# Leftover transposes of an attention pair: two parts in two successive slots of the pipeline

## The chip, the cores and the metric

One program runs on one core of a Trainium2 chip. The metric is the time of one execution on the device in microseconds (us), the median of the runs. The core has a matrix engine (PE, with its weight loads listed apart as PEld), a vector engine (DVE), a scalar engine (ACT), POOL, and SP, which here issues transfers. Each engine works through its own instructions in order, and they wait for each other by semaphores.

## What is computed

An attention with a cut at a threshold, for 8 batches of 8 heads, 576 positions and 64 columns, and then eight experts to which 4608 rows are given out greedily by their logits.

```python
scores = scale * np.matmul(q, k.transpose(0, 1, 3, 2))
thresh = np.max(scores, axis=-1, keepdims=True) - tau
scores = np.where(scores >= thresh, scores, -1000000000.0)
scores = scores - np.max(scores, axis=-1, keepdims=True)
attn = np.exp(scores)
attn = attn / (np.sum(attn, axis=-1, keepdims=True) + 1e-09)
return np.matmul(attn, v).astype(np.float32)
...
h = np.maximum(x[mask] @ w1[e], 0.0)
out[mask] = h @ w2[e]
```

## The kernel before, in words

The attention comes first and is all that the change touches; the routing and the experts follow, and start from what the last attention tiles give.

**Tiles and pairs.** Two heads make a pair `p`; there are 32 pairs, four to a batch. A pair has nine tiles of 128 query rows by 576 keys: tiles 0 to 7 are four for each head, tile 8 holds the last 64 rows of both. So there are 288 tiles, numbered through: `p,i=divmod(t,9)`.

**One tile's way.** `score` (line 69, PE) writes the scores of the tile into a score tile `sc`, `[128,2,512]` in PSUM, two banks, of which columns 0 to 287 of each bank are used. `mx` (line 74, DVE) scales it into `z` and takes the row's extreme; line 75 (POOL) adds `tau` to it. `ex` (line 86, ACT) takes the exponent into `pp` (`pm` for tile 8), and `stt` (line 90, DVE) sets to zero what lies under the threshold and sums. `tr` (line 98, PE, by the helper `turn`) transposes keys 0 to 511 of the tile into the bank tile `tb`; `trev` (lines 113 and 115, ACT) copies that into `pt`. `pv_unit` (line 144, PE) multiplies by the values into `xo`.

**The leftover.** Keys 512 to 575 are transposed apart, for the whole pair at once: `left` (by `turn`, so line 98 again, but out to `sc`) writes ten transposes into the columns from 288 on of score tiles that hold scores at the time. Its first part (n=0) is six transposes, of tiles 0 to 5; its second part (n=1) is four, two of tiles 6 and 7 and two of tile 8 (`pm`). `leftev` (ACT) copies them into `pl`: line 123 the first part (128x384), line 126 (128x128) and twice line 127 (64x64) the second. `pl_unit` (line 152, PE) multiplies `pl` by its values and closes the sum in `xo`; line 153 (ACT) copies `xo` to `xt` at the start of the next slot.

**Slots.** The loop over `s_` does two tiles of each stage in a slot: scores of tiles 2s+4 and 2s+5, `stt` of 2s+2 and 2s+3, `tr` of 2s and 2s+1, `trev` of 2s-2 and 2s-1. The order in which a slot's calls are written is the order on every engine: on PE the two scores, then units of the queue (`columns`, `whole`: `pv_unit`, `pl_unit`, units for the logits and for rows), then `tr`; on ACT first what `flush` has kept from the slot before (among it line 153), then two `trev`, then two `ex`; on DVE two `mx`, two `stt`, then copies of units. There are two score tiles (`ps_s`, bufs=2), so a slot's first score waits until the first score tile of the slot before has been read, and its second score until the second has; and one `tb` (`ps_t`, bufs=1) for both tiles of a slot, so a slot's `tr` waits for both `trev` of that slot.

**Where the leftover stands.** A pair's tile 8 is transposed by `tr` in one slot, called A here, and copied by `trev` in the next, called B. Before, both parts of `left` stand in slot B: the first behind the first score, in that score's tile; the second behind the second score, in its tile. All four copies of `leftev` stand in slot B too, ahead of both exponents. Nine slots hold two pairs. For an even `p` tile 8 is the first of its slot's two tiles, for an odd `p` the second.

Of the kernel before, what the change touches and what calls it, by code (L numbers as in the profile page):

```python
# [13 lines left out]
AF = mybir.ActivationFunctionType  # L14
# [8 lines left out]
def attention(ctx, tc, qk, vl, tau, wgd, xrows, xts, Lg, nb_batches, ident, swap, R, after_first):  # L23
# [14 lines left out]
    def load(p):  # L38
        b,j=divmod(p,4)
        x=ld.tile([128,QK],F32,name="qk"); v=ld.tile([128,2,S],F32,name="vt",bufs=VTB)  # L40
        if p==0:

            a=HS+128; h=HS+S
            for q,c,e in ((nc.sync,0,a),(nc.scalar,h,h+a),(nc.sync,a,h),(nc.scalar,h+a,QK)):
                q.dma_start(x[:,c:e], qk[b,j,:,c:e])
                if c==0: nc.sync.dma_start(taub, bass.AP(tensor=tau.tensor,offset=tau.offset,ap=[[0,128],[1,1]]))
        else: nc.sync.dma_start(x, qk[b,j])
        nc.sync.dma_start(v, vl[b,j])
        t={"v":v}; c=0
        for n,w in ((("k",0),HS),(("q",0),S),(("k",1),HS),(("q",1),S)):  # L50
            t[n]=x[:,c:c+w]; c+=w
        LD[p]=t
# [7 lines left out]
    def score(t):  # L60

        p,i=divmod(t,9); kd=LD[p]
        sc=ps_s.tile([128,2,512],F32,name="sc"); SC[t]=sc
        if i<8: todo=((i%2,slice(0,128),slice(i//2*128,i//2*128+128)),)
        else: todo=((0,slice(0,64),slice(512,576)),(1,slice(64,128),slice(512,576)))
        for h,o,c in todo:
            for f in range(2):
                r=slice(64*f,64*f+64)
                T.matmul(sc[o,f,:HS], kd["q",h][r,c], kd["k",h][r,:],start=True,stop=True)  # L69
    ZB={}  # L70
    def mx(t):
        nb=wk.tile([128,2],F32,name="nb",bufs=6); NBI[t]=nb
        z=wk.tile([128,2,HS],F32,name="z",bufs=5); ZB[t]=z
        V.tensor_scalar(z,SC.pop(t)[:,:,:HS],-0.125,None,op0=ALU.mult,op1=ALU.min,accum_out=nb[:,0:1])  # L74
        G.tensor_scalar(nb[:,1:2],nb[:,0:1],taub[:,0:1],None,op0=ALU.add)  # L75
# [3 lines left out]
    def pview(t):  # L79
        p,i=divmod(t,9)  # L80
        if i==8: return PM[p%2][:,D:D+S]
        k=(p,i//2)
        if k not in PB: PB[k]=wk.tile([128,2,S],F32,name="pp",bufs=PPB)
        return PB[k][:,place(i)]
    def ex(t):
        A.activation(pview(t),ZB[t].rearrange("p a b -> p (a b)"),AF.Exp,bias=NBI[t][:,0:1],scale=-1.0)  # L86
    def stt(t):
        p,i=divmod(t,9)
        pv=pview(t)
        V.scalar_tensor_tensor(pv,ZB.pop(t).rearrange("p a b -> p (a b)"),NBI[t][:,1:2],pv,op0=ALU.is_le,op1=ALU.mult,accum_out=den_of(p)[:,p%4,i:i+1])  # L90
# [5 lines left out]
    def turn(o,*x):  # L96
        for r in range(2):
            g=slice(64*r,64*r+64); T.transpose(o[:,r],x[r%len(x)][g],ident[g,g])  # L98
# [4 lines left out]
    def tr(t,first):  # L103
        p,i=divmod(t,9)
        tb=bank(t,first)
        pv=pview(t)
        o=(64,0) if i==8 else (64*place(i),)*2
        for kb in range(4): turn(tb[:,:,kb],*(pv[:,c+kb*128:c+(kb+1)*128] for c in o))
    def trev(t):
        p,i=divmod(t,9); tb=TB.pop(t)  # L110
        if i==0: PT[p]=wk.tile([128,2,4,S],F32,name="pt"); PL[p]=wk.tile([128,S],F32,name="pl")
        if i<8:
            A.activation(PT[p][:,i%2,:,(i//2)*128:(i//2+1)*128].rearrange("p k (r q) -> p r k q",r=2),tb,AF.Copy)  # L113
        else:
            A.activation(PT[p][:,:,:,512:576],tb,AF.Copy)
    LB={}
    def left(p,n,t):
        sc=SC[t] if t is not None else ps_s.tile([128,2,512],F32,name="sc")
        LB[p,n]=sc
        for g in ((0,1,2),(3,))[n]: turn(sc[:,:,HS+64*(g%3):HS+64*(g%3)+64],PB[p,g].rearrange("p a b -> p (a b)")[:,512:640])  # L120
        if n: turn(sc[:,:,HS+64:HS+128],PM[p%2][:,0:128],PM[p%2][:,S:S+128])
    def leftev(p,n):
        if n==0: a=LB.pop((p,0)); A.activation(PL[p][:,0:384].rearrange("p (g r q) -> p r g q",g=3,r=2),a[:,:,HS:HS+192].rearrange("p r (g q) -> p r g q",g=3),AF.Copy)  # L123
        if n==0: return
        b=LB.pop((p,1))
        A.activation(PL[p][:,384:512].rearrange("p (r q) -> p r q",r=2),b[:,:,HS:HS+64],AF.Copy)
        for r in range(2): A.activation(PL[p][64-64*r:128-64*r,512:576],b[64-64*r:128-64*r,r,HS+64:HS+128],AF.Copy)  # L127


    have={}  # L130
# [93 lines left out]
    def push_pair(p):  # L224
        b,j=divmod(p,4)
        def when(n): return lambda: have.get((p,n),1<<30)+HOLD<=st["slot"]
        if p==NP-1:


            def left(f):  # L230
                for k,g in pl_unit(p,(f,)): g(); k[0]=True
            for f in range(2):
                for u in range(4): queue.append(("c",when("t3" if f==0 else "t8"),u==0,lambda f=f,u=u: pv_unit(p,f,u),p))
                if f==0: queue.append(("n",when("t8"),False,lambda: rd_calc(b),p))
            for g in (lambda: left(0),lambda: left(1),lambda: lg_unit(b,0)(),lambda: lg_unit(b,1)(),lambda: lgt_unit(b)(),lambda: lgm_unit(b)()):
                queue.append(("n",when("pl"),False,g,p))
            queue.append(("n",lambda: not later,False,lambda: late.extend([lambda c=c: xt_unit(b,c) for c in range(5)]),p))
            return
        for f in range(2):
            for u in range(4): queue.append(("c",when("t3" if f==0 else "t8"),u==0,lambda f=f,u=u: pv_unit(p,f,u),p))  # L240
            if (f,j)==(0,3): queue.append(("n",when("t8"),False,lambda: rd_calc(b),p))
        queue.append(("c",when("pl"),False,lambda: pl_unit(p),p))
        if (b,j)==(0,0): queue.append(("n",lambda: True,False,R.consts,p))
        if (b,j)==(nb_batches-1,2): queue.append(("n",lambda: not aux,False,lambda: (R.prep(0,28),R.compare(R.k("E1"),J,0,28)),p))
        if j==3: queue.append(("n",lambda: not later,False,lambda: finish(b),p))
# [7 lines left out]
    def flush():  # L253
        for k,g in later: g(); k[0]=True
        later.clear()
    def last_slot(p): return 9*(p//2)+(12 if p%2 else 8)
    def columns(all=False):
        c=[x[4] for x in queue if x[0]=="c"]
        if not c: n=9
        else: n=9 if all else max(1,c.count(c[0])//max(1,last_slot(c[0])-st["slot"]+1))  # L260
        while queue and queue[0][1]():
            k,_,first,g,p=queue[0]
            if k=="c":
                if n==0: return
                if first and (not free_v() or (not all and not XO and len(aux)>(3 if p%2 else 0) and st["held"]!=p)): return
                n-=1
            queue.pop(0); r=g()
            if k=="c" and r:
                later.extend(r)
                return  # L270
    def whole():
        n=0
        while n<2 and aux and not XO and free_v() and st["slot"]>=st["last"]+aux[0][0]:
            r=aux.pop(0)[1](); n+=1; st["last"]=st["slot"]
            if queue: st["held"]=queue[0][4]
            later.append((banks[-1],r))
# [10 lines left out]
    for s_ in range(-2,NT//2+2):  # L287
        st["slot"]=s_
        sc_=[t for t in (2*s_+4,2*s_+5) if 0<=t<NT]; tr_=[t for t in (2*s_,2*s_+1) if 0<=t<NT]
        ev_=[t for t in (2*s_-2,2*s_-1) if 0<=t<NT]; tt_=[t for t in (2*s_+2,2*s_+3) if 0<=t<NT]  # L290
        p8=[t//9 for t in ev_ if t%9==8]
        for n in range(2):
            if n<len(sc_): score(sc_[n])
            for p in p8: left(p,n,sc_[n] if n<len(sc_) else None)

        flush()
        for t in ev_:
            p,i=divmod(t,9)
            while i==0 and p>1 and (p-2,"pv") not in have: columns(True); flush()
            trev(t); have[p,f"t{i}"]=s_  # L300
        if ev_ and ev_[-1]==NT-1: columns(True)
        for t in ev_:
            p,i=divmod(t,9)
            if i==3: push_pair(p)
            if i==8: have[p,"pl"]=s_
        for t in sc_: mx(t)
        for n in range(2):
            for p in p8: leftev(p,n)
        for t in sc_: ex(t)
        for t in tt_: stt(t)  # L310
        for t in sc_:
            p,i=divmod(t,9)
            if i==8 and p+2<NP: load(p+2)
        columns(); whole()
        for t in tr_: tr(t,t==tr_[0])
# [4 lines left out]
    for k in range(0,NBO,2):  # L320
        bk=wk.tile([128,2,4,S],F32,name="pt")
        for i in range(min(2,NBO-k)):
            b=nb_batches-NDEF-NBO+k+i; XT[b]=bk[:,i]; nc.sync.dma_start(XT[b],xts[b])
# [633 lines left out]
```

## Time and profile before

| | us |
|---|---|
| median of 3 runs | 1012.78 |
| lowest, highest of the runs | 1012.51, 1014.81 |
| the profiled execution: its own time | 1014.5 |
| its span, first to last instruction | 1012.7 |
| PE busy | 960.3 |
| PEld busy | 704.5 |
| DVE busy | 784.7 |
| ACT busy | 639.1 |
| POOL busy | 258.7 |

The trace counts from the first instruction, so the profiled execution has 1.8 us outside its span. The attention fills the span up to about 480 us: the last `tr` starts at 475.1 us, the last line 152 at 480.1 us. The rest is the routing, the first expert's start and the experts. The granted TensorE clock is 0.99 over the span.

### The profile page before, as it was taken

The numbers are of one execution on the slowest core, as the hardware profiler recorded it, in microseconds if no ns is written. First come the engines' busy times: TensorE is split into PE (matmuls) and PEld (weight loads), VectorE is DVE, ScalarE is ACT, GpSimd is POOL, SyncE is SP. The second block draws the span as 40 slices with busy tenths as digits, with TensorE's granted clock in tenths as the row PEclk, the third lists the DMA queues.
The fourth block names the chain that finished last, engine by engine and source line by source line (L and its number), as shares of the span: only waits on it lengthen the run. The fifth ranks groups of instructions, "written<-read, shape, count | busy, mean of one in ns | idle before, by whom it ended". The sixth has DMA issues, their size and how long they took to land.

```text
span 1012.7 us, 24106 instructions
## 1 busy us (share of the span) xinstructions
PE 960.3 (95%) x9141; PEld 704.5 (70%) x9141; DVE 784.7 (77%) x2158; ACT 639.1 (63%) x1257; POOL 258.7 (26%) x411
## 2 busy tenths in 40 slices
PE   7999999999999999999879999999999899999996
PEld 4555555555555555555669789797887879899895
DVE  7999999999999899997578788788687687525220
ACT  6898889788988889897745344254352444535340
POOL 2333433333333333232020222221221203220202
PEclk9999999999999999999979999999999999999999
DMA  6332424233432323202770523434343415351101
GB/s 247 98 116 83 140 81 157 99 135 124 169 115 95 102 101 118 95 26 88 245 250 13 170 97 121 136 114 128 124 138 115 143 50 177 93 174 53 42 11 41
DMA packets 35859, 116.99 MB, mean 116 GB/s; under 512 B 4384, under 2 KB 5024, under 8 KB 35232
## 3 DMA queue, kind: packets, MB, share of 16 engines
q1 hardware_dynamic: 28352, 92.85, 26.8%
q0 software_dynamic: 5888, 19.03, 6.0%
q10 hardware_dynamic: 1504, 3.59, 1.2%
q8 instruction: 72, 1.18, 0.5%
q14 instruction: 43, 0.35, 0.1%
HBM read 93.01 MB, written 21.38 MB: 113 GB/s over the span
## 4 chain that ended last, share of the span: by engine, by line
PE 69%; DVE 12%; ACT 10%; issue 6%; DMA 2%; another core or an unknown queue 0%; DVEq 0%; POOLq 0%; SPq 0%; ACTq 0%
PE pf L787 21%; PE pf L819 19%; PE xo L144 8%; PE sc L69 8%; PE tb L98 6%; DVE z L74 4%; ACT pp L86 4%; DVE pp L90 3%; ACT pt L113 3%; PE xo L152 2%; PE pt L732 2%; ACT pl L127 1%; PE rps L440 1%; PE xo L205 1%; DMA out_dram<-y,idx 1%
## 5 line engine op out<-in xcount | busy, mean ns | idle before, releaser
L75 POOL TENSOR_SCALAR nb<-nb,taub 128x1 f32<-128x1 f32 x288 | 149.4, 519 | 308.3 <-DVE z L74 257.6
L74 DVE TENSOR_SCALAR_CACHE_REDUCE z<-sc 128x576 f32<-128x576 f32 x288 | 205.9, 752 | 26.8 <-PE sc L69 14.1
L86 ACT ACTIVATE pp<-z,nb 128x576 f32<-128x576 f32 x256 | 186.4, 771 | 23.6 <-DVE z L74 23.6
L90 DVE SCALAR_TENSOR_TENSOR pp<-z,nb,pp 128x576 f32<-128x576 f32 x256 | 199.9, 813 | 0.3
L819 PE MATMUL pf<-w2h,H 128*128 128x512 f32 x576 | 195.3, 402 | 0.7 <-DVE H L372 0.7
L69 PE MATMUL sc<-qk 64*128 64x288 f32 (+1 forms) x1280 | 186.4, 427 | 7.2 <-ACT pl L123 2.7
L144 PE MATMUL xo<-pt,vt 128*64 128x320 f32 (+1 forms) x1024 | 151.1, 418 | 3.4 <-PE sc L69 1.2
L113 ACT ACTIVATE pt<-tb 128x512 f32<-128x512 f32 x256 | 139.0, 588 | 5.2 <-PE tb L98 2.2
L819 PE MATMUL pf<-w2l,H 128*128 128x512 f32 x320 | 128.3, 401 | 0.0
L826 POOL DMA_INDIRECT out_dram<-y,idx x40 | 44.6, 1115 | 314.6 <-ACT y L822 238.6
L98 PEld LDWEIGHTS tb<-ident,pp 64*128 64x128 f32 x2048 | 75.0, 139 | 69.6 <-ACT pt L113 28.0
L819 PEld LDWEIGHTS pf<-w2h,H 128*128 128x128 f32 x576 | 106.5, 189 | 20.2 <-DVE H L372 1.6
L69 PEld LDWEIGHTS sc<-qk 64*128 64x128 f32 (+1 forms) x1280 | 91.1, 178 | 34.3 <-ACT pl L127 9.0
L787 PE MATMUL pf<-xh,w1h 128*128 128x288 f32 (+2 forms) x512 | 110.7, 303 | 0.7 <-ACT xh L733 0.7
L144 PEld LDWEIGHTS xo<-pt,vt 128*64 128x64 f32 x1024 | 63.4, 136 | 68.4 <-issue 34.7
L787 PE MATMUL pf<-xh,w1l 128*128 128x288 f32 (+2 forms) x512 | 110.7, 302 | 0.0
L787 PE MATMUL pf<-xl,w1h 128*128 128x288 f32 (+2 forms) x512 | 110.6, 302 | 0.0
L98 PE MATMUL tb<-ident,pp 64*128 64x64 f32 x2048 | 93.9, 229 | 12.3 <-ACT pt L113 12.0
L822 ACT ACTIVATE y<-pf 128x512 f32<-128x512 f32 x40 | 23.9, 598 | 129.3 <-PE pf L819 121.1
L799 ACT ACTIVATE hf<-pf 128x576 f32<-128x576 f32 x56 | 36.5, 652 | 93.2 <-PE pf L787 80.3
L787 PEld LDWEIGHTS pf<-xh,w1h 128*128 128x128 f32 x512 | 82.6, 191 | 1.5 <-ACT xh L733 1.1
L787 PEld LDWEIGHTS pf<-xh,w1l 128*128 128x128 f32 x512 | 82.6, 191 | 0.2
(199 smaller groups left out, 1311.4 us busy)
## 6 DMA issues: line engine op xcount, KB each, us to landing
qk<-qk_dram SPq DMA_DIRECT2D x31, 864.0 KB, 4.9
vt<-vl_dram SPq DMA_DIRECT2D x32, 576.0 KB, 3.8
w2s<-w_dram SPq DMA_DIRECT2D x32, 512.0 KB, 5.3
w1s<-w_dram SPq DMA_DIRECT2D x28, 512.0 KB, 4.3
xrows<-pp SPq DMA_DIRECT2D x24, 260.0 KB, 2.3
xts<-xt SPq DMA_DIRECT2D x2, 1152.0 KB
pt<-xts SPq DMA_DIRECT2D x2, 1152.0 KB, 7.9
xrows<-xr SPq DMA_DIRECT2D x8, 260.0 KB, 2.4
```

The source lines that it names most:

```text
L69: T.matmul(sc[o,f,:HS], kd["q",h][r,c], kd["k",h][r,:],start=True,stop=True)
L74: V.tensor_scalar(z,SC.pop(t)[:,:,:HS],-0.125,None,op0=ALU.mult,op1=ALU.min,accum_out=nb[:,0:1])
L75: G.tensor_scalar(nb[:,1:2],nb[:,0:1],taub[:,0:1],None,op0=ALU.add)
L86: A.activation(pview(t),ZB[t].rearrange("p a b -> p (a b)"),AF.Exp,bias=NBI[t][:,0:1],scale=-1.0)
L90: V.scalar_tensor_tensor(pv,ZB.pop(t).rearrange("p a b -> p (a b)"),NBI[t][:,1:2],pv,op0=ALU.is_le,op1=ALU.mult,accum_out=den_of(p)[:,p%4, ...
L98: g=slice(64*r,64*r+64); T.transpose(o[:,r],x[r%len(x)][g],ident[g,g])
L113: A.activation(PT[p][:,i%2,:,(i//2)*128:(i//2+1)*128].rearrange("p k (r q) -> p r k q",r=2),tb,AF.Copy)
L144: T.matmul(xo[64*h:64*h+64,:q.stop-q.start],v[:,f,128*u+64*h:128*u+64*h+64],PT[p][:,h,u,q],start=(u==0),stop=False,skip_group_check=True)
L787: T.matmul(ps[:,h,:n],s[w][:,k,f*128:(f+1)*128],s[x][:,k,cols[h]],start=(i==0),stop=(i==11))
L799: A.activation(hf,ps[:,:,:HS],AF.Relu)
L819: T.matmul(ps[:,0,:],H[:,f,c:c+128],s[w][:,f],start=(f==0 and j==0),stop=e)
L826: G.indirect_dma_start(out=out,out_offset=IOA(ap=s["idx"][:n,t:t+1],axis=0),in_=y[:n],in_offset=None)
```

## The change

The first part of `left` moves from slot B to slot A, behind both scores of that slot, and writes into the second score's tile. The second part stays in slot B behind both scores, in the second score's tile as before. `leftev` follows its part: line 123's copy now stands in slot A and lines 126 and 127 in slot B, each between the two exponents of the slot. The work itself, its shapes and its number are the same.

```diff
-        p8=[t//9 for t in ev_ if t%9==8]
-        for n in range(2):
-            if n<len(sc_): score(sc_[n])
-            for p in p8: left(p,n,sc_[n] if n<len(sc_) else None)
+        p8=[(t//9,n) for n,x in enumerate((tr_,ev_)) for t in x if t%9==8]
+        for t in sc_: score(t)
+        for p,n in p8: left(p,n,sc_[-1] if sc_ else None)
...
         for t in sc_: mx(t)
-        for n in range(2):
-            for p in p8: leftev(p,n)
-        for t in sc_: ex(t)
+        for t in sc_[:1]: ex(t)
+        for p,n in p8: leftev(p,n)
+        for t in sc_[1:]: ex(t)
```

`leftev` is written anew with the same four copies; lines from there on shift by two, later by one, so line 123 becomes 125, lines 126 and 127 become 127 and 128, and lines 144 and 152 become 146 and 154.

On PE, this is the start of slot A of an even pair before (the names in brackets are the semaphores waited for):

```order
L69 MATMUL sc<-qk 128x288 [waits DVE_49]
L69 MATMUL sc<-qk 128x288
L69 MATMUL sc<-qk 128x288 [waits DVE_49]
L69 MATMUL sc<-qk 128x288
L144 MATMUL xo<-pt,vt 64x320 x4
```

and now:

```order
L69 MATMUL sc<-qk 128x288 [waits DVE_49]
L69 MATMUL sc<-qk 128x288
L69 MATMUL sc<-qk 128x288 [waits DVE_49]
L69 MATMUL sc<-qk 128x288
L98 MATMUL sc<-ident,pp 128x64 x6
L146 MATMUL xo<-pt,vt 64x320 x4
```

The six transposes of the first part have come in behind the two scores and ahead of the multiplication by the values. The same pair's slot B on PE before (`pm_101` is its tile 8):

```order
L69 MATMUL sc<-qk 128x288 [waits DVE_49]
L69 MATMUL sc<-qk 128x288
L98 MATMUL sc<-ident,pp 128x64 x6
L69 MATMUL sc<-qk 128x288 [waits DVE_49]
L69 MATMUL sc<-qk 128x288
L98 MATMUL sc<-ident,pp 128x64 x2
L98 MATMUL sc<-ident,pm_101 128x64 x2
```

and now:

```order
L69 MATMUL sc<-qk 128x288 [waits DVE_49]
L69 MATMUL sc<-qk 128x288
L69 MATMUL sc<-qk 128x288 [waits Activation_49]
L69 MATMUL sc<-qk 128x288
L98 MATMUL sc<-ident,pp 128x64 x2
L98 MATMUL sc<-ident,pm_101 128x64 x2
```

They have gone from between the two scores of slot B, whose second score now waits for a copy of ACT's: the first part's, in slot A.

On ACT, slot B of an even pair and the first copies of the slot behind it, before:

```order
L115 ACTIVATE pt<-tb 128x8x64 [waits PE_49]
L113 ACTIVATE pt<-tb 128x2x4x64 [waits Activation_49]
L123 ACTIVATE pl<-sc 128x2x3x64 [waits DVE_49]
L126 ACTIVATE pl<-sc 128x128 [waits DVE_49]
L127 ACTIVATE pl<-sc 64x64 x2
L86 ACTIVATE pp<-z,nb 128x576 x2
L113 ACTIVATE pt<-tb 128x2x4x64 [waits PE_49]
L113 ACTIVATE pt<-tb 128x2x4x64
```

and now, from the exponents of slot A on (line 178, 176 before, is a copy for the logits that `flush` has kept):

```order
L86 ACTIVATE pp<-z,nb 128x576 [waits DVE_49]
L125 ACTIVATE pl<-sc 128x2x3x64 [waits DVE_49,Activation_49]
L86 ACTIVATE pp<-z,nb 128x576
L178 ACTIVATE lt<-xo 128x320 [waits PE_49]
L115 ACTIVATE pt<-tb 128x8x64 [waits PE_49]
L113 ACTIVATE pt<-tb 128x2x4x64 [waits Activation_49]
L86 ACTIVATE pp<-z,nb 128x576 [waits DVE_49]
L127 ACTIVATE pl<-sc 128x128 [waits DVE_49]
L128 ACTIVATE pl<-sc 64x64 x2
L86 ACTIVATE pp<-z,nb 128x576
L113 ACTIVATE pt<-tb 128x2x4x64 [waits PE_49]
L113 ACTIVATE pt<-tb 128x2x4x64
```

In slot B one exponent now stands ahead of the copies of the leftover and one behind, and the largest of the copies is gone to slot A, between that slot's exponents. The first score of the slot behind B, which waited for ACT's line 123, now waits for DVE's `mx` alone. The order on DVE is the same in both kernels, and so are the transfers of SP and the work of POOL.

More of the change, by code (lines that the diff above doesn't have):

```diff
@@ L122, in leftev @@
     def leftev(p,n):
[L123 to L127, printed above, removed]
+        sc=LB.pop((p,n))
+        if n==0:
+            A.activation(PL[p][:,0:384].rearrange("p (g r q) -> p r g q",g=3,r=2),sc[:,:,HS:HS+192].rearrange("p r (g q) -> p r g q",g=3),AF.Copy)
+            return
+        A.activation(PL[p][:,384:512].rearrange("p (r q) -> p r q",r=2),sc[:,:,HS:HS+64],AF.Copy)
+        for r in range(2): A.activation(PL[p][64-64*r:128-64*r,512:576],sc[64-64*r:128-64*r,r,HS+64:HS+128],AF.Copy)
     have={}
```

## The prediction

> **What bounds the kernel now.** I read the table by stretches first, then the groups of the page, the list of waits, the chain of waits, and last the timeline of one slot B and the slot behind it. The columns of the stretch: its length, then busy time and count of PE, PEld, DVE, ACT and POOL, the granted clock, the transfers' share and GB/s.
>
> ```profile
> 25.00:475.00 450.00, 431.27 (x5157) 251.15 (x5157) 425.10 (x1211) 392.57 (x750) 150.72 (x294) 1.00 0.31 104
> L74 DVE TENSOR_SCALAR_CACHE_REDUCE z<-sc 128x576 f32<-128x576 f32 x288 | 205.9, 752 | 26.8 <-PE sc L69 14.1
> PE tb L98 <- ACT pt L113: 8.3, 22, 0.6
> PE sc L69 <- ACT pl L123: 2.5, 4, 0.8
> PE sc L69 <- ACT pl L127: 1.3, 8, 0.2
> PE tb L98 <- ACT pt L113: 1.4, 5, 0.5
> ```
>
> In the attention PE is busy 431 of 450 us and DVE 425: two engines near full that take turns in setting the pace. The second row says where DVE loses time: 26.8 us of idle time ahead of line 74, over the whole span, waiting for PE. The last four are PE's waits (total, times, longest); the first three hold for 60 to 470 us, the last for 25 to 60 us. PE idles 8.3 us in 22 waits ahead of the transposes into `tb`, for ACT's copies out of it.
>
> ```profile
> 449.30 0.50 ACT pl L123
> ...
> 451.22 0.76 ACT pp L86
> 451.98 0.97 ACT pt L113 x2
> 452.99 0.71 PE tb L98 x16
> ```
>
> The chain that ended last runs through this place: line 123's copy, the other copies of the leftover, an exponent, two copies of `pt`, then `tb`. So ACT's work in slot B does set the end, though ACT as a whole is the emptiest of the three.
>
> **One slot B and the slot behind it.** Start, length, what; in brackets the idle time ahead and who ended it.
>
> ```profile
> 402.59 0.76 DVE L74 TENSOR_SCALAR_CACHE_REDUCE z<-sc 128x576 f32<-128x576 f32 x1 [0.67 <-PE sc L69]
> 407.16 0.76 DVE L74 TENSOR_SCALAR_CACHE_REDUCE z<-sc 128x576 f32<-128x576 f32 x1
> 407.85 0.08 DVE L74 DVE_READ_ACCUMULATOR z<-sc 128x1 f32 x1
> 407.96 0.49 ACT L123 ACTIVATE pl<-sc 128x384 f32<-128x384 f32 x1 [2.15 <-DVE z L74]
> 408.64 0.28 ACT L126 ACTIVATE pl<-sc 128x128 f32<-128x128 f32 x1 [0.19 <-DVE z L74]
> 408.93 0.45 ACT L127 ACTIVATE pl<-sc 64x64 f32<-64x64 f32 x2
> 409.28 1.43 ACT L86 ACTIVATE pp<-z,nb 128x576 f32<-128x576 f32 x2
> 410.61 1.06 ACT L113 ACTIVATE pt<-tb 128x512 f32<-128x512 f32 x2
> 408.50 0.76 PE L69 MATMUL sc<-qk 64*128 64x288 f32 x4 [0.76 <-ACT pl L123]
> 409.43 0.71 PE L69 MATMUL sc<-qk 64*64 64x288 f32 x8 [0.17 <-ACT pl L127]
> 410.07 1.08 PE L144 MATMUL xo<-pt,vt 128*64 128x256 f32 x8
> 411.72 0.71 PE L98 MATMUL tb<-ident,pp 64*128 64x64 f32 x16 [0.56 <-ACT pt L113]
> 412.27 1.19 PE L69 MATMUL sc<-qk 64*128 64x288 f32 x8
> 413.39 1.30 PE L144 MATMUL xo<-pt,vt 128*64 128x320 f32 x8
> ```
>
> The copies of the leftover hold ACT from 407.96 to 409.38; both exponents follow, from 409.28; only then come the two copies of `pt`, done at 411.67, and `tb` starts at 411.72. PE could have started it at 411.08: its work of line 144 ends at 411.15, and a group starts some 0.07 us before the end of the one ahead (412.27 + 1.19 = 413.46, the next starts at 413.39). This wait so costs 0.56 + 0.07 = 0.63 us.
>
> **The change, part by part.** No work is added or taken away; four things move.
>
> The exponent ahead of the copies. The first exponent needs `z` alone. The first row's accumulator has been read at 407.93, so it starts at 407.96, where line 123 starts now. One exponent takes the queue for 1.43 - 0.76 = 0.67 us, to 408.63: the time at which line 126 starts anyway, once the second `z` is done (408.64). Lines 126 and 127 stay where they are, to 409.38; the second exponent starts at 409.28, where the first does now; the copies of `pt` start 0.67 us earlier, at 409.94, and end at 411.00; ACT would allow `tb` at 411.05, PE at 411.08. The second score keeps its wait for line 127 (409.43). So `tb` starts at 411.08, and the whole wait of 0.63 us is gone; ACT has given 0.67, so no wait of these 22, whose longest is 0.6, is left. **8.3 + 22 x 0.07 = 9.8 us** of PE time.
>
> Whether PE's time is the kernel's. A while later stand slot A and slot B of the next pair, an odd one, in whose slot B `z` waits for PE:
>
> ```profile
> 415.16 1.19 PE L69 MATMUL sc<-qk 64*128 64x288 f32 x8
> 416.60 0.75 DVE L74 TENSOR_SCALAR_CACHE_REDUCE z<-sc 128x576 f32<-128x576 f32 x1
> 418.21 0.71 ACT L153 ACTIVATE xt<-xo 128x256 f32<-128x256 f32 x2
> 418.76 0.70 PE L69 MATMUL sc<-qk 64*128 64x288 f32 x4
> 419.30 0.34 PE L98 MATMUL sc<-ident,pp 64*128 64x64 f32 x6
> 419.48 0.70 PE L69 MATMUL sc<-qk 64*128 64x288 f32 x4
> 419.46 0.59 ACT L115 ACTIVATE pt<-tb 128x512 f32<-128x512 f32 x1
> 419.68 0.76 DVE L74 TENSOR_SCALAR_CACHE_REDUCE z<-sc 128x576 f32<-128x576 f32 x1 [0.84 <-PE sc L98]
> 420.07 0.23 PE L98 MATMUL sc<-ident,pm 64*128 64x64 f32 x2
> 420.37 0.75 DVE L74 TENSOR_SCALAR_CACHE_REDUCE z<-sc 128x576 f32<-128x576 f32 x1
> 421.25 0.71 PE L98 MATMUL tb<-ident,pp 64*128 64x64 f32 x16
> 424.24 0.71 PE L98 MATMUL tb<-ident,pp 64*128 64x64 f32 x16 [0.24 <-ACT pt L113]
> ```
>
> From 411.72 to 419.30 no PE row has a wait, so 0.63 us gained at the first comes out at the last, and the 0.84 us of DVE's wait there is long enough to take it. What is late next is PE's own work, with 0.21 us of the wait left. Behind odd pairs it is the same on a smaller scale: 0.24 + 0.07 = 0.31 us at 424.24 comes out at the next slot A, where `z` waits 0.67 us for PE (as at 402.59). I take these 9.8 us as fully paid. Of the five waits before 60 us (1.4 us) I count 0.6 us, from the nearest rows an estimate between nothing and 1.4 + 5 x 0.07 = 1.8: there DVE hardly ever idles.
>
> The first part moved ahead in PE's queue. Between two scores its six transposes push the next group back 419.48 - 419.30 = 0.18 us, though their row is 0.34 long. They push slot A's later work back by this and B's scores too; B's second score no longer has them ahead of it. For B's first `z`: now 419.30 + 0.34 = 419.64 must be done; then the score alone, at 418.76 + 0.18 + 0.70 = 419.64. Nothing won or lost. For B's second `z` the last transpose ends at 420.07 + 0.23 = 420.30 either way, and it starts at 420.37: 0.07 us to spare. In slot A the second `z` now waits for the first part too: the scores end at 415.16 + 1.19 = 416.35. At 419.30 the six transposes end 0.18 us after the score ahead of them (418.76 + 0.70 = 419.46), so here at 416.53; the `z` starts at 416.60, 0.07 to spare again. I take nothing for both. The other end: the whole row of 0.34 us exposed in 32 slots A, 10.9 us, and 0.23 us in 32 slots B, 7.4 us. A gain from them is excluded, since the transposes stand ahead of either `z` in PE's order.
>
> The first part's copy in slot A. It goes behind the first exponent and ends before the second score of slot B (0.49 us after the second `z`, over 1 us ahead). What is behind it on ACT, the second exponent, the two copies of line 153 and the copies of `pt`, comes up to 0.49 us later. At 419.46 the last of these ends at 420.05; `tb` starts at 421.25. Of these 1.2 us, 0.49 go for the copy and 0.63 for PE's lead: 0.08 us are left, so I take nothing. The other end is 0.49 - 0.08 = 0.41 us in 16 slots, 6.6 us. DVE's own queue has the same rows in the same order.
>
> **The sum.** 9.8 + 0.6 = **10.4 us**. The profiled execution took 1014.5 us, so 1004.1; the median of the runs shown, 1012.78, is 1.7 lower, so **1002.4 us**. DVE's whole idle time ahead of line 74, 26.8 us, is a ceiling for any gain of this kind; 16.4 us of it stay.
>
> A page of the Trainium skill speaks against this sum. Perfetto Trace Analysis, section "Identifying the Most-Contended Engine", says that matmul busy time is a poor measure, that the weight loads' share is the better one, and that the most contended engine is to be improved. By it PE (weight loads 251 of 450 us) has room, DVE with 425 of 450 is the engine, and a change that leaves DVE's rows alone would bring nothing: the second rival below. The waits of `z` for PE, 0.84 us at 419.68, say otherwise for the slots that count.
>
> The clock is another matter:
>
> ```profile
> 510.00:514.00 4.00, 3.69 (x42) 3.52 (x42) 3.54 (x11) 0.00 (x0) 0.00 (x0) 0.57 0.49 133
> 520.00:534.00 14.00, 10.32 (x46) 9.45 (x47) 9.90 (x28) 5.73 (x14) 3.13 (x4) 0.52 0.68 220
> ```
>
> After the attention PE is granted 0.57 and 0.52 in two stretches. Were the second a quarter (3.5 us) longer or shorter, PE would lose or win about half of that, 1.7 us by the 0.52; the three runs shown lie 2.3 us apart as it is. This stays inside the range. TensorE: Matmul & The Clock Gate, section "Part 1: The HAM clock gate", says why it could: the gate is set by free-running windows of 3.413 us, so an earlier end of the attention meets them elsewhere. By it the sum is 1.7 us more or less per window; no run here shows it yet.
>
> **The rivals.**
> *ACT gives part of it back.* The copy in slot A makes `tb` of slot B late behind odd pairs. For it: only 0.08 us to spare. Against: 1.2 us of room before. Price 6.6 us: 1002.4 + 6.6 = 1009.0; half of it would be 1005.7.
> *DVE is the bound, PE's lead is lost.* The waits of `z` for PE come back as others. For it: DVE busy 94% of the attention. Against: 0.84 and 0.67 us of idle time just there. No change, 1012.8.
> *Slower: the second `z` waits for the transposes.* Place: the second `z` of slots A and B, where 0.07 us is to spare; from the point where the transposes end later than that, each us is DVE's. With both whole rows exposed, 10.9 + 7.4 = 18.3 us against 10.4: 7.9 slower, 1020.7. Against: a row of 0.34 costs the next group only 0.18.
> *More.* PE's waits for line 123 and 127 (2.5 + 1.3 us) come on top, where I have them inside the same slots' gain: 1002.4 - 3.8 = 998.6.
> That the change does not do what it says is excluded by the order of the rows.
>
> **How the numbers follow.** Forecast 0.62, ACT's part 0.15, no change 0.09, slower 0.07, more 0.07. A measurement tells about 0.3%, 3 us, from no change. Faster by over 0.3%: 0.62 + 0.15 + 0.07 = 0.84 (ACT's whole price still leaves 3.8 us); the same 0.09; slower 0.07. The range runs from the case of more, 998.6, to ACT's whole price, 1009.0; it leaves out no change and slower, 0.16.
>
> **What would show it.** Right: no wait of `tb` for `pt` behind slots B; the first `z` of an odd pair's slot B waits 0.2 us for PE instead of 0.84 where the `tb` ahead had waited 0.56, and about 0.5 where it had waited less; DVE's idle time ahead of line 74 down from 26.8 to about 16 us. ACT's rival: `tb` of slot B waits for `pt` behind line 155's copies. DVE's rival: fewer waits of PE, the same length of slots. Slower: an idle time ahead of each second `z`, put down to the transposes. Wrong: a gain that does not lie before 480 us.

## The result, and the profile after

| | before | after |
|---|---|---|
| median of four runs each, run side by side, us | 1013.79 | 1002.01 |
| lowest to highest, us | 1012.51 to 1015.33 | 1001.47 to 1004.09 |
| profiled execution, its own time, us | 1014.5 | 1002.47 |
| its span, us | 1012.7 | 1000.6 |
| start of the last pair of `z` rows in the trace, us | 468.24 | 457.45 |
| from there to the end of the span, us | 544.48 | 543.16 |

The ratio is **0.9887, with an interval of 0.9865 to 0.9909**: 11.8 us faster. The last pair of `z` rows (line 74) closes the stretch in which the order of the change holds. It comes **10.8 us earlier**; what follows is 1.3 us shorter.

The kernel after in the table by stretches: the length, busy time and count of PE, PEld, DVE, ACT and POOL, the granted clock, the transfers.

```profile
25.00:475.00 450.00, 438.86 (x5266) 261.80 (x5263) 426.76 (x1229) 392.27 (x769) 152.27 (x295) 1.00 0.32 110
```

The group of line 74 on its page, with the idle time ahead of it at the end:

```profile
L74 DVE TENSOR_SCALAR_CACHE_REDUCE z<-sc 128x576 f32<-128x576 f32 x288 | 205.5, 749 | 19.8 <-PE sc L69 19.2
```

And PE's waits from 60 to 470 us (total, times, longest):

```profile
PE sc L69 <- ACT pl L128: 4.5, 8, 0.7
...
PE tb L98 <- ACT pt L113: 0.3, 1, 0.3
```

The 450 us of the stretch reach 17.6 us past the last pair of `z` rows here and 6.8 us past it before, so its busy times are not of the same work. From 25 us to that pair PE is busy for 422.3 of 432.4 us, and before for 425.4 of 443.2: its idle time fell from 17.8 to 10.1 us. The 22 waits of `tb` for `pt`, 8.3 us before, are down to one of 0.3 us. A wait that was only 0.2 us long in each case has grown: the second score of slot B waits for line 128 (127 before), 4.5 us in eight slots.

The slot B that the prediction took apart now stands at 398 us. Its timeline on DVE, ACT and PE, each row with start, length, instruction, and in brackets the idle time ahead:

```profile
398.11 0.76 DVE L74 TENSOR_SCALAR_CACHE_REDUCE z<-sc 128x576 f32<-128x576 f32 x1
398.91 0.77 ACT L86 ACTIVATE pp<-z,nb 128x576 f32<-128x576 f32 x1 [1.70 <-DVE z L74]
399.59 0.27 ACT L127 ACTIVATE pl<-sc 128x128 f32<-128x128 f32 x1
399.88 0.45 ACT L128 ACTIVATE pl<-sc 64x64 f32<-64x64 f32 x2
400.23 0.76 ACT L86 ACTIVATE pp<-z,nb 128x576 f32<-128x576 f32 x1
400.89 1.06 ACT L113 ACTIVATE pt<-tb 128x512 f32<-128x512 f32 x2
400.38 0.71 PE L69 MATMUL sc<-qk 64*64 64x288 f32 x8 [0.69 <-ACT pl L128]
401.02 1.08 PE L146 MATMUL xo<-pt,vt 128*64 128x256 f32 x8
402.04 0.71 PE L98 MATMUL tb<-ident,pp 64*128 64x64 f32 x16
```

The copies of `pt` now end at 401.95, and `tb` starts at 402.04 with no wait: PE's own line 146 ends at 402.10. The score that waits for line 128 comes no later than before: it starts 400.38 - 398.11 = 2.27 us behind the first `z` of the slot, as it did at 409.43 - 407.16. Its wait is longer because PE, which line 123 no longer holds up, is there sooner. From the first `z` of the slot to the `tb` of the slot behind it was 411.72 - 407.16 = 4.56 us before; it is 402.04 - 398.11 = **3.93 us** now. I call this distance the yardstick, since every experiment below has a slot B in which it can be read.

### The profile page after: what moved, and what is told of

Same layout as the page of the kernel before. It is cut to its first block, busy times and chain, and to the rows that moved or that the text cites. A ratio compares the mean times of both kernels' runs of the same rounds, so it can differ in the third digit from the quotient of the medians.

```text
span 1000.6 us, 24121 instructions
## 1 busy us (share of the span) xinstructions
PE 956.1 (96%) x9141; PEld 707.6 (71%) x9141; DVE 781.3 (78%) x2158; ACT 632.2 (63%) x1257; POOL 258.2 (26%) x411
## 4 chain that ended last, share of the span: by engine, by line
PE 81%; DVE 8%; ACT 4%; issue 4%; DMA 2%; another core or an unknown queue 0%; POOLq 0%; SPq 0%; DVEq 0%; ACTq 0%
PE pf L788 21%; PE pf L820 19%; PE sc L69 12%; PE xo L146 12%; PE tb L98 7%; PE xo L154 2%; DVE pp L90 2%; PE pt L733 2%; DVE z L74 2%; ACT pp L86 2%; PE xo L207 1%; DVE cmp L373 1%; PE rps L441 1%; DMA out_dram<-y,idx 1%; PE xo L173 1%
## 5 line engine op out<-in xcount | busy, mean ns | idle before, releaser
L86 ACT ACTIVATE pp<-z,nb 128x576 f32<-128x576 f32 x256 | 193.2, 773 | 47.4 <-DVE z L74 46.5
L74 DVE TENSOR_SCALAR_CACHE_REDUCE z<-sc 128x576 f32<-128x576 f32 x288 | 205.5, 749 | 19.8 <-PE sc L69 19.2
L69 PE MATMUL sc<-qk 64*128 64x288 f32 (+1 forms) x1280 | 180.9, 425 | 8.3 <-ACT pl L128 4.7
L69 PEld LDWEIGHTS sc<-qk 64*128 64x128 f32 (+1 forms) x1280 | 93.2, 178 | 39.7 <-ACT pl L128 13.2
```

## The experiments

My theory (Q in the expectations) is the prediction's: the gain is ACT's time ahead of `pt` in slot B, and it takes both parts of the change, the exponent ahead of the copies and the first part's copy out of slot B. The rivals: one of the parts alone does it, because a score stops waiting for line 123 (S), or because the six transposes leave their place ahead of a `z` of slot B (P). Four kernels ran on one chip beside 12 runs of the kernel before, with a median there of 1007.98 us; four more on another chip beside 16 runs, with a median of 1012.87 us.

**The changed kernel again.** The reference for the other three on this chip.

> The changed kernel once more, for its spread and a second look at the granted clock. Theory Q (the queue: the gain is that on ACT one exponent and the first part's copy no longer stand between the second z of slot B and the copies of pt): 1001 to 1004 us, no wait of tb for pt behind slots B, attention shorter by 10 to 11 us. If a part of the gain was the clock's (one stretch of half clock instead of two, 13.7 us instead of 17.1), the stretches may come out otherwise here, and the time would move by up to 2 us with them.

It took 996.98 us, ratio 0.9894 [0.9879, 0.9909]. The last `z` pair starts at 457.41 us, 0.04 us from the first trace. So the start of that pair holds to a few hundredths between these two traces, while the part behind it does not: 536.85 us here, 543.16 us in the first trace. The experiments are therefore read by the start of the last pair, and by the whole time only as a second witness.

**The order alone.** The kernel before, with all four copies still in slot B, but behind its first exponent.

```diff
-        for n in range(2):
+        for t in sc_[:1]: ex(t)
+        for n in range(2):
             for p in p8: leftev(p,n)
-        for t in sc_: ex(t)
+        for t in sc_[1:]: ex(t)
```

> Before, with one thing changed: all four copies of the leftover stand between the two exponents of slot B instead of ahead of both; PE's order is that of before. Theory Q: the copies of pt start earlier by one exponent (0.67) less what the copies are pushed back by (0.39 for line 123), 0.26 us, so of each of the 22 waits of tb 0.25 us goes: 5 to 7 us faster than before, about 1007. Rival S (the gain is that the first score behind slot B no longer waits for line 123's copy): that wait gets longer by 0.67 us in 8 slots, so 1013 to 1019. Rival P (the gain is that the first z of slot B no longer waits for the six transposes): no change, 1013.

It took 1003.07 us, ratio 0.9946 [0.9932, 0.9959]; the last pair starts at 463.39 us, 4.85 us earlier than before. PE's waits of this kernel from 60 to 470 us, and then its slot B on three engines:

```profile
PE sc L69 <- ACT pl L123: 7.9, 8, 1.4
...
PE tb L98 <- ACT pt L113: 0.3, 1, 0.3
```

```profile
403.16 0.76 DVE L74 TENSOR_SCALAR_CACHE_REDUCE z<-sc 128x576 f32<-128x576 f32 x1
403.96 0.78 ACT L86 ACTIVATE pp<-z,nb 128x576 f32<-128x576 f32 x1 [2.15 <-DVE z L74]
404.65 0.47 ACT L123 ACTIVATE pl<-sc 128x384 f32<-128x384 f32 x1
405.17 1.40 PE L69 MATMUL sc<-qk 64*128 64x288 f32 x12 [1.43 <-ACT pl L123]
407.52 0.71 PE L98 MATMUL tb<-ident,pp 64*128 64x64 f32 x16
```

Here too `tb` no longer waits, but the wait has only moved. Line 123 still reads the first score tile of slot B, now 0.69 us later, and the next score into that tile stands still for 1.43 us instead of 0.76. The yardstick is 407.52 - 403.16 = 4.36 us: 0.2 of the 0.63 us. By the last pair this is a little less than half of the 10.8 us, by the ratio about half of the gain. The expectation had the size and not the way: the waits of `tb` were to shrink by 0.25 us each; they went, and the wait for line 123 grew from 2.5 to 7.9 us, as rival S had said.

**The move alone.** The changed kernel, with the copies ahead of both exponents of their slots.

```diff
-        for t in sc_[:1]: ex(t)
         for p,n in p8: leftev(p,n)
-        for t in sc_[1:]: ex(t)
+        for t in sc_: ex(t)
```

> The changed kernel with the copies of the leftover ahead of both exponents again, in slot A and in slot B; the transposes and their places are those of the changed kernel. Theory Q: in slot B the copies of pt wait for the second z, 0.75 us of copies and two exponents as before, so the waits of tb come back nearly whole: 1010 to 1015 us. Rivals S and P: all of the gain stays, about 1002.

It took 1010.03 us, ratio 1.0021 [1.001, 1.0031]; the last pair starts at 470.41 us, 2.2 us *later* than before. Of PE's waits from 60 to 470 us:

```profile
PE tb L98 <- ACT pt L113: 9.8, 21, 0.6
```

One of DVE's waits from 25 to 470 us:

```profile
DVE rm L181 <- ACT lt L178: 2.6, 5, 0.7
```

And its slot B:

```profile
408.82 0.76 DVE L74 TENSOR_SCALAR_CACHE_REDUCE z<-sc 128x576 f32<-128x576 f32 x1
410.30 0.28 ACT L127 ACTIVATE pl<-sc 128x128 f32<-128x128 f32 x1 [1.72 <-DVE z L74]
410.59 0.45 ACT L128 ACTIVATE pl<-sc 64x64 f32<-64x64 f32 x2
410.94 1.43 ACT L86 ACTIVATE pp<-z,nb 128x576 f32<-128x576 f32 x2
413.39 0.72 PE L98 MATMUL tb<-ident,pp 64*128 64x64 f32 x16 [0.56 <-ACT pt L113]
```

The largest copy is gone from slot B, and nothing is won by it: the first copy that is left waits for the *second* `z`, and both exponents stand behind it. ACT idles where line 123 was. The yardstick is 413.39 - 408.82 = 4.57 us, that of before, although no score waits for line 123 and no first `z` of a slot B waits for the transposes any more. With this S and P fall as causes that would do alone. The 2.2 us come mostly from slots A of even pairs, which are 1.8 us longer in sum: four of them by 0.45 us each and the others not at all. In these four DVE's line 181, a small copy for the logits, waits about 0.5 us for ACT's line 178, which stands behind the exponents and so behind the first part's copy. The fifth wait, of 0.7 us, was there before too. The parts do not add up: -4.9 and +2.2 us alone, -10.8 us together. The exponent has to stand ahead so that it fills the time before the second `z`, and line 123 has to be gone so that it does not come behind that exponent.

**The six transposes in slot A's first score tile.** The changed kernel, with the first part between the two scores of slot A.

```diff
-        for t in sc_: score(t)
-        for p,n in p8: left(p,n,sc_[-1] if sc_ else None)
+        for m in range(2):
+            if m<len(sc_): score(sc_[m])
+            for p,n in p8:
+                if n==m: left(p,n,sc_[n] if n<len(sc_) else None)
```

> The changed kernel with the six transposes of slot A between its two scores, in the first score's tile, instead of behind both in the second's; their copy and the exponents stand as in the changed kernel. Theory Q: the queue of ACT is the same, so nearly all of the gain stays: 1002 to 1005 us, the 0 to 3 us from the first z of slot A, which now waits 0.18 us longer where it waits for PE. Rival P (what counts is that no first z waits for the six transposes): most of the gain is lost, 1010 to 1013.

It took 997.79 us, ratio 0.9904 [0.9889, 0.9919], an interval that overlaps that of the changed kernel beside it. The last pair starts at 459.75 us, 2.3 us later than in the changed kernel. Here the first `z` of a slot A:

```profile
395.49 0.76 DVE L74 TENSOR_SCALAR_CACHE_REDUCE z<-sc 128x576 f32<-128x576 f32 x1 [0.84 <-PE sc L98]
```

It idles for 0.84 us where slots A of even pairs idled for 0.67 both before (402.59) and after. In 12 of the slots ahead of a slot A of an even pair the length grows by 0.16 to 0.18 us, 2.1 us in all. So six transposes ahead of a `z` that waits cost 0.17 us, half of their row of 0.34. The yardstick stays at 3.9 us at the place taken apart.

**One more copy in slot B.** To the changed kernel comes a copy of 128x384 on ACT behind the second part's copies, into a tile that nothing reads.

```diff
+    dm=cst.tile([128,3,128],BF16,name="dm")
...
-        for p,n in p8: leftev(p,n)
+        for p,n in p8:
+            leftev(p,n)
+            if n==1: A.activation(dm,ident.unsqueeze(1).to_broadcast([128,3,128]),AF.Copy)
```

> The changed kernel with one more copy on ACT in slot B, behind the copies of the second part and ahead of the second exponent: 384 columns from SBUF to a tile that nobody reads, about 0.4 us. It uses no bank and no result of PE or DVE. Theory Q: the copies of pt start 0.4 us later; in the 8 places where the wait of tb was 0.56 us it comes back by 0.4, in the 14 others, where ACT had 0.25 to 0.3 us to spare, by about 0.1: 3 to 5 us slower than the changed kernel, ratio to before about 0.993 to 0.994. Rivals S and P: no change, 0.989 to 0.990.

It took 1007.99 us, ratio 0.9942 [0.9923, 0.9962]; the last pair starts at 462.63 us, 5.2 us later than in the changed kernel. PE's waits from 60 to 470 us, then the copy (line 312) and what follows in one slot B:

```profile
PE tb L98 <- ACT pt L113: 3.5, 11, 0.4
```

```profile
402.53 0.76 DVE L74 TENSOR_SCALAR_CACHE_REDUCE z<-sc 128x576 f32<-128x576 f32 x1
404.65 0.51 ACT L312 ACTIVATE dm<-ident 128x384 bf16<-128x384 f32 x1
405.06 0.76 ACT L86 ACTIVATE pp<-z,nb 128x576 f32<-128x576 f32 x1
406.84 0.71 PE L98 MATMUL tb<-ident,pp 64*128 64x64 f32 x16 [0.31 <-ACT pt L113]
```

The copy takes 405.06 - 404.65 = 0.41 us of ACT's queue, and the yardstick becomes 406.84 - 402.53 = 4.31 us, 0.38 more than after. Here nearly the whole copy is paid, as in all eight places where the wait of `tb` had been 0.56 us: ACT has no spare time there, as the prediction's 411.05 against 411.08 said. Elsewhere it has some: behind most slots B of odd pairs the yardstick grows by only 0.13 us, from 4.18 to 4.31. The 5.2 us lie just above the 3 to 5 expected.

**The same copy in slot A.** As above, with `n==0` in place of `n==1`.

> The same extra copy in slot A instead, behind the first part's copy and ahead of the second exponent. By the prediction's step on slot A only 0.08 us were to spare there, so about 0.3 us in 16 slots would be lost, 5 us; by the trace of the changed kernel, where the copies of pt end 0.45 us ahead of tb in the one slot B looked at, nothing is lost: ratio 0.989 to 0.990. If it is ACT's total load that counts and not the place, both kernels with the copy lose the same.

It took 1004.44 us, ratio 0.9915 [0.9883, 0.9947]; the last pair starts at 460.63 us, 3.2 us later than in the changed kernel. It settled for neither expectation. The kernel's waits: PE's from 60 to 470 us, DVE's from 25 to 480 us, and one of the latter in the timeline.

```profile
PE tb L98 <- ACT pt L113: 1.0, 3, 0.4
```

```profile
DVE z L74 <- PE sc L69: 15.8, 32, 0.9
DVE rm L181 <- ACT lt L178: 6.4, 6, 5.0
```

```profile
328.71 0.68 ACT L178 ACTIVATE lt<-xo 128x256 f32<-128x256 f32 x2
329.10 0.34 DVE L181 COPY rm<-xo 64x4 f32<-64x4 f32 x2 [0.47 <-ACT lt L178]
```

`tb` gives only 0.7 us more of waits. Another 1.4 us are DVE's: five short waits of line 181 for ACT's line 178, the pair that cost the move alone its 1.8 us, where the changed kernel has only the long one at the end. The prediction names no such consumer of ACT's queue behind slot A. The lengths of the slots ahead of slot A of even pairs, whose end is the first `z` there, grow by 1.0 us, and those of slots A of even pairs by 0.9 us. The rest of the 3.2 us is spread over small amounts, whose causes stay open.

**The six transposes twice.** The changed kernel, which in slot A writes the same transposes a second time.

```diff
-        for g in ((0,1,2),(3,))[n]: turn(
+        for g in ((0,1,2,0,1,2),(3,))[n]: turn(
```

> The changed kernel with the six transposes of slot A done twice, to the same place. It prices them: if they cost PE 0.18 us as taken in the prediction, and PE sets the pace from slot B to the next, about 0.2 us in 14 slots A of odd pairs and up to as much in even ones, 3 to 6 us slower than the changed kernel; if the whole row of 0.34 us counts (the slower rival's price), 5 to 11 us, with an idle time ahead of the second z of slot A put down to line 98.

It took 1004.51 us, ratio 0.9918 [0.9889, 0.9948]; the last pair starts at 462.25 us, 4.8 us later than in the changed kernel. First a slot A of the changed kernel on PE, then the same slot with the transposes doubled, on PE and DVE:

```profile
392.79 1.19 PE L69 MATMUL sc<-qk 64*128 64x288 f32 x8
393.82 0.34 PE L98 MATMUL sc<-ident,pp 64*128 64x64 f32 x6
394.09 0.66 PE L185 MATMUL xo<-ident,lt 128*128 128x128 f32 x4
```

```profile
397.72 0.53 PE L98 MATMUL sc<-ident,pp 64*128 64x64 f32 x12
398.18 0.66 PE L185 MATMUL xo<-ident,lt 128*128 128x128 f32 x4
...
398.13 0.08 DVE L74 DVE_READ_ACCUMULATOR z<-sc 128x1 f32 x1
398.29 0.76 DVE L74 TENSOR_SCALAR_CACHE_REDUCE z<-sc 128x576 f32<-128x576 f32 x1
```

Six more add 0.53 - 0.34 = 0.19 us to the row and as much to PE's queue: 398.18 - 397.72 = 0.46 us to the next group, where it was 0.27. The second `z` of this slot starts 0.08 us after the accumulator of the first has been read (398.21), where it had started at once; such a delay is there in 13 slots A of even pairs. Later, in slots B of odd pairs, the first `z` idles for 0.19 us more, 0.54 instead of 0.35 at the place shown below. Summed, slots A of odd pairs are 2.9 us longer (about 0.19 us in each of 15) and slots A of even pairs 2.2 us (0.17 us in each of those 13). So **PE's time is the kernel's here at about its full price**, and the 0.07 us to spare that the prediction gave the second `z` are used up by 0.19 us more.

**Three parts in three slots.** The changed kernel, with the leftover in three parts: the first goes into the slot ahead of A, the two transposes of tiles 6 and 7 into A, and those of `pm` stay in B, each with its copies.

```diff
+        for g in ((0,1,2),(3,),())[n]: turn(
...
+        if n==2: turn(sc[:,:,HS:HS+64],PM[p%2][:,0:128],PM[p%2][:,S:S+128])
...
-        p8=[(t//9,n) for n,x in enumerate((tr_,ev_)) for t in x if t%9==8]
+        p8=[(t//9,n) for n,x in enumerate((tt_,tr_,ev_)) for t in x if t%9==8]
```

> The changed kernel with the leftover in three slots: tiles 0 to 5 one slot ahead of A, tiles 6 and 7 in A, tile 8 in B. ACT then has 0.45 us of copies in slot B in place of 0.75. Theory Q: in the 8 places where the second score waits for ACT's last copy and ACT and PE now allow tb at the same time, both come 0.3 us earlier: up to 2.4 us faster than the changed kernel, ratio to before 0.987. If PE's own work is the bound there already, no change, 0.989 to 0.990.

It took 1000.18 us, ratio 0.9882 [0.985, 0.9915], and the last pair starts at 457.48 us, 0.03 us from the changed kernel. PE's waits from 60 to 470 us, where line 130 is what 128 was:

```profile
PE sc L69 <- ACT pl L130: 3.3, 8, 0.5
```

The score's wait for ACT falls by 1.2 us. The yardstick at the same place, and the first `z` of the slot A ahead of it:

```profile
393.50 0.76 DVE L74 TENSOR_SCALAR_CACHE_REDUCE z<-sc 128x576 f32<-128x576 f32 x1 [0.86 <-PE sc L69]
...
398.08 0.76 DVE L74 TENSOR_SCALAR_CACHE_REDUCE z<-sc 128x576 f32<-128x576 f32 x1
...
401.84 0.71 PE L98 MATMUL tb<-ident,pp 64*128 64x64 f32 x16
```

The yardstick is 401.84 - 398.08 = 3.76 us, 0.17 less than in the changed kernel, and slots A of odd pairs are 1.6 us shorter in sum, so a gain from slot B is there, if less than the 2.4 us named. It is lost in another place. The six transposes now stand one slot ahead of A, where the multiplication behind the scores starts 1.30 us after them in place of 1.12, and behind this the first `z` of a slot A of an even pair waits 0.86 us for PE where it waited 0.67. The slots ahead of these slots A are 1.9 us longer in sum. It is the price of the transposes once more, 0.19 us at this place, and by chance it takes back what the shorter copies had won. No version here is shown to beat the changed kernel.

## Why the prediction was right, step by step

**The waits of `tb`, 9.8 us, and the early ones, 0.6.** Right in size and cause. The yardstick fell by 0.63 us at the place taken apart, exactly as worked out (411.72 to 411.08). The attention is 10.8 us shorter, 10.4 were forecast. It holds place by place too: from 60 us on, where `tb` had waited 0.56 us behind a slot B of an even pair, the three slots up to the next slot B are 0.61 to 0.63 us shorter together, and 0.34 to 0.40 where it had waited 0.26 to 0.40. Behind odd pairs seven of the eight waits gave 0.37 to 0.41, where 0.31 was forecast, and one place without such a wait gave 0.47, where DVE's wait of 0.7 us for ACT's line 176 went. Ahead of 60 us 0.6 us were gained; that this estimate between nothing and 1.8 came out so well is luck. Both halves of the argument were tried: without the exponent ahead (the move alone) the wait stays at 0.56 us, and with line 123 left in slot B (the order alone) it moves to a score.

**Where the gain comes out.** Half right. The prediction let the whole 0.63 us come out at the first `z` of the odd pair's slot B, which was to wait 0.2 us. That `z` after, and one between the two slots B, both from DVE's timeline; then the same place between them in the kernel before:

```profile
403.17 0.81 DVE L90 SCALAR_TENSOR_TENSOR pp<-z,nb,pp 128x576 f32<-128x576 f32 x1
403.91 0.75 DVE L74 TENSOR_SCALAR_CACHE_REDUCE z<-sc 128x576 f32<-128x576 f32 x1
...
410.01 0.76 DVE L74 TENSOR_SCALAR_CACHE_REDUCE z<-sc 128x576 f32<-128x576 f32 x1 [0.35 <-PE sc L69]
```

```profile
412.22 0.81 DVE L90 SCALAR_TENSOR_TENSOR pp<-z,nb,pp 128x576 f32<-128x576 f32 x1
...
413.02 0.76 DVE L74 TENSOR_SCALAR_CACHE_REDUCE z<-sc 128x576 f32<-128x576 f32 x1
```

The `z` at 410.01 waits 0.35 us, not 0.2: it gained 0.49. From 80 us on it waits, in the seven places behind a wait of 0.56 us, 0.35 to 0.48 us and in the six behind shorter ones 0.62 to 0.70, where 0.2 and about 0.5 had been named. Before, the `z` at 413.02 started 0.80 us after line 90's row; now 0.74 us lie between the two. It had been late for PE by 0.06 us, and no view listed this as idle time, since the row ahead was still ending. Over the attention, slots A of odd pairs are 4.8 us shorter, the two slots between each even pair's slot B and the next slot A 2.6 us, the slots ahead of slots A of even pairs 1.5 us, and the rest 2.0 us; together 10.9 us, with a start 0.1 us later.

**DVE's idle time ahead of line 74.** Wrong by a third of the fall: 26.8 us were to fall to about 16, and it is 19.8. The gain is there all the same, because of the hidden lateness just shown. From the first `z` to the last pair DVE's idle time fell by 7.9 us; line 74's rows took 2.9 us less of DVE's queue beyond that (from the end of the row ahead to their own), while their own mean fell only from 752 to 749 ns. A "ceiling" taken from idle time alone was therefore too low in principle.

**The six transposes in PE's queue, taken at nothing.** Right. They cost PE's queue 0.17 us (first tile) and 0.19 us (doubled) per six, 0.18 was used. In slot A they end at 393.82 + 0.34 = 394.16, and the second `z` starts at 394.23 as fast as it can: the 0.07 us forecast. With this the slower case falls; the doubled kernel shows where it would have begun.

**The first part's copy in slot A, taken at nothing.** Right in its result and wrong in its margin. The rows of ACT and PE at the odd pair's slot B, where 0.08 us was to be left:

```profile
408.27 0.49 ACT L125 ACTIVATE pl<-sc 128x384 f32<-128x384 f32 x1
408.66 0.77 ACT L86 ACTIVATE pp<-z,nb 128x576 f32<-128x576 f32 x1
...
410.38 0.62 ACT L115 ACTIVATE pt<-tb 128x512 f32<-128x512 f32 x1
...
411.51 0.71 PE L98 MATMUL tb<-ident,pp 64*128 64x64 f32 x16
```

The copies end at 411.00 and `tb` starts at 411.51: 0.5 us are left. Two terms were too large. The copy takes the queue for the 408.66 - 408.27 = 0.39 us from its start to the next, and not for its row of 0.49, as I had counted. Of the 1.2 us of before, 1.2 - 0.39 - 0.51 = 0.3 us are then left for PE's lead here, in place of 0.63. A second copy in slot A still cost 3.2 us, and with it came 1.4 us of waits of line 181 for line 178, which the prediction did not name.

**The rivals.** *ACT gives part back*: no, by the margin above. *DVE is the bound*: no, 10.8 us. The prediction took it from the Trainium skill, Perfetto Trace Analysis, "Identifying the Most-Contended Engine", which advises improving the fullest engine first and judging the matrix engine's headroom by its weight loads (and by MFU, the share of peak that its arithmetic reaches). By weight loads DVE is the fullest here: from 25 us to the last `z` pair it was busy for 419 of 443 us before and 416 of 432 after, the weight loads for 248 and 253. That a change which leaves DVE's rows alone would bring nothing is the prediction's own step from there and not the section's; it fails, since PE's waits were worth nearly their whole length. *More*: no. The waits of scores for ACT did not vanish, they grew to 4.5 us, and the attention ended as forecast without them; shortening them to 3.3 us (three parts) was worth 1.6 us in slots A of odd pairs, which the moved transposes took back.

**The clock.** PE's stretch at half clock after the attention in the kernel after (length first, the granted clock behind the counts):

```profile
508.18:521.83 13.65, 10.76 (x48) 9.79 (x49) 10.44 (x29) 5.73 (x14) 3.18 (x4) 0.50 0.71 224
```

It is one stretch of 13.65 us; before there were two, 17.07 us together. The attention's 10.8 us and this part's 1.3 us make the 12.1 us between the two spans. The 1.3 us lie inside the ±1.7 us that the prediction allowed, and were not part of its sum; the part behind the attention differs by more than that between two traces of the changed kernel, so they are no gain of this change that is shown. The second time the changed kernel gained 1007.98 - 996.98 = 11.0 us on the runs beside it.

## What to carry to other kernels

- When two instructions stand ahead of a critical copy in one queue, ask which of them can already run while the other waits for its input; here the exponent needed the first `z` alone, and two of the three lines of copies that stood ahead of it needed the second.
- Taking an instruction out of such a queue wins nothing while the one behind it waits for a later event anyway (line 126 for the second `z`), and reordering alone hands the wait to whoever needs the instruction that was pushed back: read both, and try both alone.
- Size a margin on an in-order queue by the distance from start to start and not by the row's length, and list every consumer behind the place, small copies too.

## What the runs showed of the hardware

PE's time at half clock (granted 0.50) behind the attention came in steps of 3.41 us in every trace: 10.24, 13.65, 17.07 or 20.48 us. The last 4 to 7 us of every span, at half clock too, are left out; the kernels with the copy have one of their steps at some 785 us, among the experts. In the table, "rest" is the time from the last `z` pair to the end of the span.

| chip | kernel | half clock, us | rest, us |
|---|---|---|---|
| first | six transposes in first tile | 10.24 | 535.93 |
| first | changed kernel again | 13.65 | 536.85 |
| first | move alone | 13.65 | 536.51 |
| first | order alone | 17.07 | 538.41 |
| second | transposes twice | 13.65 | 538.79 |
| second | three parts | 13.65 | 540.41 |
| second | copy in slot A | 17.07 | 540.96 |
| second | copy in slot B | 20.48 | 543.84 |

On the first chip two steps more go with 2.5 us, on the second with 3.4 to 5.1 us: between 1.2 and 2.5 us for each of two steps on average; single steps lie between 0.6 and 2.9 us. The step agrees with the Trainium skill, TensorE: Matmul & The Clock Gate, "Part 1: The HAM clock gate", which gives free-running windows of 3.413 us. That the steps cause the whole of these differences was not tried; two traces with the same 13.65 us on the second chip differ by 1.6 us. The changed kernel itself has 13.65 us in both of its traces, and a rest of 543.16 us and 536.85 us, so the 6 us between these two have another cause, which stays open.
